# An explicit order of operations, bf16 loads and DMA transposes in an RWKV-7 scan with a feed-forward layer

## The chip, the cores and the metric

The kernel runs on one core of a Trainium2 chip. The metric is the device time of one execution in microseconds (us). "TensorE" below is the matmul engine (PE in the profile, PEld for its weight loads), VectorE is DVE, ScalarE is ACT, GpSimd is POOL, and SyncE is SP, which here only issues transfers. PSUM is where TensorE's results arrive; an "evacuation" is the copy of a result from there to SBUF, where the operands lie.

## The reference, cut to what matters

The first half is a recurrence over 768 steps with a 40x40 state for each of 4 x 8 heads. The second half sends the 3072 resulting rows through two matrices with a softplus between them.

```python
for t in range(S):                                   # S = 768, B = 4, H = 8, D = 40
    y[:, :, t] = np.einsum('bhd,bhde->bhe', rt, state)
    Sa = np.einsum('bhde,bhe->bhd', state, at)
    state = state * wt[:, :, None, :] - np.einsum('bhd,bhe->bhde', Sa, bt)
    state = state + np.einsum('bhd,bhe->bhde', vt, kt)
...
x = y.transpose(0, 2, 1, 3).reshape(B * S, H * D)    # 3072 x 320
h = x @ w_in                                         # 320 x 2048
g = np.maximum(h, 0.0) + np.log1p(np.exp(-np.abs(h)))
return g @ w_out                                     # 2048 x 320
```

## The kernel before

The sequence is cut into 12 chunks of 64 steps. Two chunks make a window. Per window a 32x32 triangular system per (head, parity) is inverted with elementwise operations (`invert`). Per chunk the operands are scaled, transposed, multiplied into Gram matrices and chained through the state (`second`); most of these are 64x64 matmuls (in the profile of this kernel 32 of them, at 207 us, take 0.37 us to the next group's start). Then come the feed-forward products with full 128x128 weights (`mlp`).

The program does not write instructions in a fixed order. It builds a graph of some 1,800 operations, and a greedy scheduler picks their order, engine and PSUM bank from modelled durations. One part of that model matters for this study, and I did not see that when I predicted: it has TensorE's instructions fetched in blocks of 256 (the profile below shows 63 instruction packets of 16 KB for 16032 TensorE instructions), and the scheduler charges for a block that arrives too late. The operations named in `SLOW` (feed-forward products, which are long for their instruction count: 0.11 us a matmul, start to start, at 204 us, where the 64x64 ones above take 0.012) are put where the model waits for a block.

```python
DVE_FW = (0, 1)                    # windows whose inverse runs on DVE, the others on GpSimd
BY_DMA = {"k": 99, "v": 99, "r": 99, ...}    # from which chunk on a transpose is made by DMA: never
...
BLOCK, AHEAD, FETCH, BEFORE = 256, 82, 2300.0, 70
SLOW = ("h", "o", "csb")

class Fetch:                       # the model of TensorE's instruction fetch
    def run(self, start, cost, n, keep=False):
        ...
        while left:
            edge = (at // BLOCK + 1) * BLOCK
            ask = edge - AHEAD
            ...
            if at == edge:
                w = max(0.0, asked + FETCH - t)      # the stall at the edge of a block
                stall += w
                t += w
...
# in schedule(): a stall is a penalty, and a long operation is wanted while a block is on its way
if e == "pe":
    pen += fetch.run(s + pen, c, 2 * COUNT[o.name])
    if o.name in SLOW:
        want = FILL if fetch.wants(s) else -SAVE
...
key = want - o.due - PEN * pen - 3.0 * cost * (len(o.engines) > 1)
```

A transpose is 8 matmuls of 128x128. The values v and r arrive as f32 over SyncE or ScalarE, and GpSimd casts them:

```python
def f(e):                          # transpose
    for bp in X2:
        for yy in range(H_ // 2):
            i = T.transpose(pb(t)[:, bp, off + 128 * yy:off + 128 * yy + 128],
                            src[:, bp, 128 * yy:128 * yy + 128], ident[:, :])
...
for n, dst, dn in (("v", v_, vn), ("r", r_, rn)):            # in second(c)
    src = RAW[n](c)[0]
    op(pool(640 * 0.85), landed(RAW[n], c), [dn],
       lambda e, dst=dst, src=src: P.tensor_copy(hd(dst), bh(src, D_)), name="cast")
turned(c, ("k", k_, [kn], kT_, kTn), ("v", v_, [vn], vT_, vTn))
turned(c, ("r", r_, [rn], rT_, rTn))
```

## Time and profile before

| | before |
|---|---|
| median of 3 runs | 351.06 us (348.99 to 351.34) |
| span of the profiled run | 345.8 us |
| first feed-forward matmul | 77.3 us |
| TensorE instructions (8016 matmuls, each with a weight load) | 16032 |

The prediction below shows the busy table, the table of stretches and the start. Four more lines of the page turned out to matter. They are the granted TensorE clock in 40 slices of the span (tenths of full speed), the DMA's busy share in the same slices, the queue of kind "instruction" (packets, MB, share of the 16 DMA engines), and the shares of the chain of work that ended last:

```profile
PEclk9967865569999978999899999999999999999999
DMA  8999984687667565676546465430411400100101
q8 instruction: 63, 1.03, 1.2%
PE 47%; ACT 11%; POOL 9%; DMA 9%; SPq 9%; DVE 7%; issue 5%; ACTq 2%; DVEq 0%; POOLq 0%
```

The clock is at 9 nearly everywhere from the tenth slice on. The third line is easily passed over, with 63 packets and 1.2% of the DMA. But 16032 TensorE instructions / 256 = 62.6, so I read these packets as TensorE's program arriving in blocks of 256 instructions (b_quart, further down, has 19488 / 256 = 76.1, and 76 packets). "issue" in the last line is time for which the profile names nothing to wait for. It is 5% of the chain here.

### The profile page before, as it was taken

Reading aid. Unit: us, or ns where it says so; the run is one execution under the profiler, and the core shown is the slowest. Engines: PE = TensorE matmul, PEld = TensorE weight load, DVE = VectorE, ACT = ScalarE, POOL = GpSimd, SP = SyncE. Lnnn points to the kernel's source line nnn. Section 1 sums busy time; section 2 is a strip of 40 time slices with the busy share of each in tenths; the row PEclk is TensorE's granted clock in tenths of the full one; section 3 lists DMA queues with packets and bytes.
Section 4 is the critical chain, followed back from the end, with each engine's and each line's share of the span. In section 5 each row is a group of like instructions: output and inputs, shape, how many; then the busy total and the mean of one; then the engine's idle time right before and its main releaser. Section 6 shows DMA issues by size and latency. Waiting matters only on the chain.

```text
span 345.8 us, 17638 instructions
## 1 busy us (share of the span) xinstructions
PE 280.4 (81%) x8016; PEld 212.7 (61%) x8016; DVE 232.7 (67%) x419; ACT 210.3 (61%) x296; POOL 169.2 (49%) x309
## 2 busy tenths in 40 slices
PE   0337247688789969999799999998989899999873
PEld 0226126576567747777577776786766678777642
DVE  7729978889997746657756697585885656664201
ACT  1246704226797825877568888667687368667661
POOL 8106000001000627898888788898888888000000
PEclk9967865569999978999899999999999999999999
DMA  8999984687667565676546465430411400100101
GB/s 134 171 174 142 182 159 79 107 145 113 122 120 156 103 112 94 123 126 108 102 79 104 83 104 96 78 69 14 89 34 21 91 14 13 33 6 21 39 22 38
DMA packets 145787, 31.30 MB, mean 90 GB/s; under 512 B 140272, under 2 KB 145392, under 8 KB 145712
## 3 DMA queue, kind: packets, MB, share of 16 engines
q1 hardware_dynamic: 129504, 25.09, 42.9%
q10 hardware_dynamic: 13728, 2.46, 5.1%
q0 software_dynamic: 2480, 2.62, 4.7%
q8 instruction: 63, 1.03, 1.2%
q14 instruction: 12, 0.10, 0.1%
HBM read 28.84 MB, written 3.93 MB: 95 GB/s over the span
## 4 chain that ended last, share of the span: by engine, by line
PE 47%; ACT 11%; POOL 9%; DMA 9%; SPq 9%; DVE 7%; issue 5%; ACTq 2%; DVEq 0%; POOLq 0%
PE ps L1205 12%; PE ps L1224 12%; SPq L664 8%; PE ps L730 7%; POOL mt L971 4%; DMA wout<-in_moe_w_out_dram 3%; POOL mtmp L967 3%; ACT gT L1214 3%; ACT et L1211 3%; PE ps L773 2%; DMA a_f<-in_a_dram 2%; PE ps L1073 2%; ACTq L664 2%; DMA r_f<-in_r_dram 2%; PE ps L1174 2%
## 5 line engine op out<-in xcount | busy, mean ns | idle before, releaser
L1205 PE MATMUL ps<-xT,win 128*128 128x256 bf16 x576 | 79.9, 275 | 3.5 <-ACT et L1211 1.8
L1211 ACT ACTIVATE et<-ps 128x512 f32<-128x512 f32 x96 | 57.2, 596 | 36.3 <-PE ps L1205 35.8
L967 POOL TENSOR_TENSOR mtmp<-mt 128x30 f32<-128x30 f32 (+14 forms) x120 | 60.5, 504 | 33.0 <-DVE mt L960 24.3
L971 POOL TENSOR_TENSOR mt<-mt,mtmp 128x30 f32<-128x30 f32 (+14 forms) x120 | 66.8, 557 | 8.7
L1224 PE MATMUL ps<-wout,gT 128*128 128x320 bf16 x384 | 65.2, 302 | 5.9 <-ACT gT L1214 2.9
L1205 PEld LDWEIGHTS ps<-xT,win 128*128 128x128 bf16 x576 | 50.6, 98 | 15.9 <-ACT et L1211 6.0
L1214 ACT ACTIVATE gT<-et,hln 128x1024 bf16<-128x1024 f32 x48 | 55.2, 1151 | 1.4
L1224 PEld LDWEIGHTS ps<-wout,gT 128*128 128x128 bf16 x384 | 34.2, 98 | 20.1 <-ACT gT L1214 4.6
L1035 POOL CAST r_b<-r_f 128x640 bf16<-128x640 f32 x12 | 9.5, 789 | 44.2 <-DMA r_f<-in_r_dram 39.6
L1035 POOL CAST v_b<-v_f 128x640 bf16<-128x640 f32 x12 | 9.2, 765 | 37.0 <-DMA v_f<-in_v_dram 24.8
L1229 DVE TENSOR_TENSOR osb<-ps,csb 128x320 f32<-128x320 f32 x24 | 11.6, 484 | 20.3 <-PE ps L1224 20.1
L785 DVE TENSOR_TENSOR qt<-ps,sut 128x1024 bf16<-128x1024 f32 x12 | 14.6, 1221 | 5.6 <-PE ps L773 5.6
L814 PE MATMUL ps<-lw,nexc 64*64 64x320 bf16 x96 | 7.2, 361 | 13.8 <-ACT lw L845 13.6
L814 PE MATMUL ps<-lw,ninc 64*64 64x320 bf16 x96 | 9.8, 328 | 8.5 <-ACT ginv L862 6.2
L785 DVE TENSOR_TENSOR tak<-ps,sut 128x1024 bf16<-128x1024 f32 x12 | 14.6, 1219 | 2.8 <-PE ps L773 2.6
L785 DVE TENSOR_TENSOR pt<-ps,sut 128x1024 bf16<-128x1024 f32 x12 | 14.6, 1216 | 2.6 <-PE ps L773 2.6
L1180 DVE TENSOR_TENSOR yo<-ps,gexc 128x640 bf16<-128x640 f32 x12 | 9.9, 821 | 8.3 <-PE ps L1174 8.2
L845 ACT ACTIVATE lw<-w_f 128x1280 bf16<-128x1280 f32 x6 | 7.7, 1282 | 12.3 <-DMA w_f<-in_w_dram 12.3
L868 DVE TENSOR_TENSOR kh<-k_f,ginv 128x640 bf16<-128x640 f32 x12 | 10.9, 910 | 4.8 <-DMA k_f<-in_k_dram 4.8
L985 ACT ACTIVATE dex<-dc,blk 128x1024 bf16<-128x1024 bf16 x6 | 6.9, 1146 | 11.6 <-DVE dc L979 11.6
L866 DVE SCALAR_TENSOR_TENSOR nh<-b_f,ginv 128x640 bf16<-128x640 f32 x12 | 9.9, 825 | 5.3 <-ACT ginv L862 5.3
L862 ACT ACTIVATE ginv<-ps 128x640 f32<-128x640 f32 x12 | 8.4, 704 | 8.0 <-issue 6.8
(152 smaller groups left out, 587.9 us busy)
## 6 DMA issues: line engine op xcount, KB each, us to landing
out_dram<-osb SPq DMA_DIRECT2D x48, 80.0 KB, 2.3
b_f<-in_b_dram SPq DMA_DIRECT2D x44, 80.0 KB, 3.6
v_f<-in_v_dram SPq DMA_DIRECT2D x44, 80.0 KB, 3.3
a_f<-in_a_dram SPq DMA_DIRECT2D x44, 80.0 KB, 3.4
k_f<-in_k_dram SPq DMA_DIRECT2D x44, 80.0 KB, 3.6
r_f<-in_r_dram SPq DMA_DIRECT2D x42, 80.0 KB, 3.1
w_f<-in_w_dram SPq DMA_DIRECT2D x20, 160.0 KB, 4.2
wout<-in_moe_w_out_dram POOLq DMA_DIRECT2D x4, 320.0 KB, 10.0
```

The source lines that it names most:

```text
L664: lambda e, bp=bp, x=x, q=q: queue(e).dma_start(heads(t[q:q + 64, bp, :], D_), SRC[n][2 * bp + x][:, c * L:(c + 1) * L, :].rearrange("h p ...
L730: i = T.transpose(pb(t)[:, bp, off + 128 * yy:off + 128 * yy + 128], src[:, bp, 128 * yy:128 * yy + 128], ident[:, :])
L785: lambda e: V.tensor_tensor(parity(dst), bh(pf(t), L), bc4(mask[:, :], L), ALU.mult), name="mask")
L814: i = T.matmul(pf(t)[s:s + 64, bp, 0:DM], mats[z][q:q + 64, :], heads(lwt[q:q + 64, bp, :], 2 * D_)[:, :, z * D_:z * D_ + D_], start=(z == ...
L967: lambda e, j=j, nt=nt, tv=tv: E_.tensor_tensor(tv, m[:, 0:j, j:j + 1].to_broadcast([128, j, nt]), m[:, j:j + 1, j + 1:32].to_broadcast([1 ...
L971: lambda e, j=j, tv=tv: E_.tensor_tensor(m[:, 0:j, j + 1:32], m[:, 0:j, j + 1:32], tv, ALU.add),
L1035: lambda e, dst=dst, src=src: P.tensor_copy(hd(dst), bh(src, D_)), name="cast")
L1205: i = T.matmul(one(t)[:, 256 * (q % 2):256 * (q % 2) + 256], win[:, z, q * 128:(q + 1) * 128], xT_[:, z, :], start=(z == 0), stop=(z == 2))
L1211: lambda e, q2=q2, t=t, ett=ett: A.activation(ett[:, q2 % 2, :], one(t), AF.Exp), name="exp")
L1214: lambda e, q2=q2, ett=ett: A.activation(gts[q2 // 2][0][:, :, :].rearrange("p q m -> p (q m)"), ett[:, :, :].rearrange("p q m -> p (q m)" ...
L1224: i = T.matmul(one(t)[:, 0:DM], gts[z][0][:, q % 4, bp * 128:(bp + 1) * 128], wout[:, q, :], start=(q == 0), stop=(q == NQ - 1))
L1229: lambda e, t=t, ot=ot: V.tensor_tensor(ot[:], one(t)[:, 0:DM], csb[:], ALU.add), name="oe")
```

## The change

The intent is to take work off TensorE (transposes by DMA, cheaper transposes, fewer switches between 64x64 and 128x128 mode), to take the casts off GpSimd by letting its DMA cast, to share the inverses between GpSimd and DVE, and to replace the greedy scheduler by an explicit order found by a local search. The scheduler goes, and its model of instruction fetch goes with it; whether the search had such a model, the file does not say.

```diff
-DVE_FW = (0, 1)
+DVE_FW = (0, 1, 3, 5)
-FIRST = [...]; BY_ACT = (...); TUNED = {...}      # (cut)
-BY_DMA = {"k": 99, "v": 99, "r": 99, "u": 99, "a": 99, "n": 99}
+BY_DMA = {"k": 4, "v": 4, "r": 4, "u": 99, "a": 99, "n": 99}
+ORDER = (2, 110, 3, 70, 32, 33, ...)              # 1792 numbers (cut)
+ENGINE = "..."; BANK = "..."                      # (cut)
+QUARTERS = "101011111111111010111100111111111101111011111100"
...
-class Fetch: ...
-def schedule(ops): ...
+def arrange(ops):
+    for o, q in zip((o for o in ops if o.alt), QUARTERS):
+        o.mode = o.alt[0] if q == "1" else o.mode
+    for at, n in enumerate(ORDER):
+        o = ops[n]
+        o.eng = names[ENGINE[n]]
+        ...                                        # PSUM banks from BANK (cut)
+    return [ops[n] for n in ORDER]
...
-        r_b = Ring("r_b", 1, [128, 2, 512], BF)
+        r_b = Ring("r_b", 2, [128, 2, 512], BF)
...
+        def load_cast(n, c):                       # v and r, by GpSimd, f32 -> bf16
+            ...
+                    op({"pool": 700.0}, [], [nm + "%d%d" % (bp, x)],
+                       lambda e, bp=bp, x=x, q=q: P.dma_start(
+                           heads(t[q:q + 64, bp, :], L)[:, :, 0:D_],
+                           SRC[n][2 * bp + x][:, c * L:(c + 1) * L, :].rearrange("h p d -> p h d")),
+                       dma=(nm + "%d%d" % (bp, x), 512))
...
         def transpose(src, srcs, t, off):
+                        for q in (0, 64) if mode == QUAD else ():
+                            for o in (0, 64):
+                                i = T.transpose(pb(t)[o:o + 64, q // 64, n:n + 64],
+                                                src[q:q + 64, bp, 128 * yy + o:128 * yy + o + 64], eye(q))
```

A "quarter" transpose is thus 32 matmuls of 64x64 where a "whole" one is 8 of 128x128. Of the 48 transposes left on TensorE, 38 are by quarters. The two counts that follow from this are 8736 matmuls instead of 8016, and 171 mode switches instead of 243.

> **What bounds the kernel now.** I read the page's busy table first, then the table of stretches, then the timeline of the start and of a stretch in the middle.
>
> The busy table: TensorE (PE) is the busiest engine, and no other is near it.
>
> ```profile
> PE 280.4 (81%) x8016; PEld 212.7 (61%) x8016; DVE 232.7 (67%) x419; ACT 210.3 (61%) x296; POOL 169.2 (49%) x309
> ```
>
> The table of stretches (start:end, length, busy time of each engine, granted clock, DMA share, GB/s) shows that this average hides two regimes. I cut the span where the first matmul of the feed-forward part (L1205) starts, at 77.3 us, and where the tail begins.
>
> ```profile
> 0.00:40.00 40.00, 15.20 (x304) 10.57 (x304) 28.37 (x93) 17.55 (x23) 14.54 (x39) 0.87 1.12 158
> 40.00:77.00 37.00, 23.31 (x766) 18.70 (x768) 31.25 (x64) 10.22 (x13) 2.17 (x3) 0.58 0.77 127
> 77.00:320.00 243.00, 224.44 (x6782) 171.82 (x6767) 169.74 (x258) 170.49 (x245) 152.50 (x267) 0.98 0.45 80
> 320.00:346.00 26.00, 17.47 (x191) 11.60 (x188) 3.35 (x6) 12.03 (x16) 0.00 (x0) 0.97 0.15 33
> ```
>
> In the first 77 us PE is busy 38.5 us and idle as long; VectorE (DVE) is busy 59.6 of 77 and the DMA is saturated until 40. From 77 to 320 us PE is busy 224 of 243 us: here the time is PE's own work plus 18.6 us of gaps. The tail of 26 us is the last chunk's exp, ln and output product in turn.
>
> The timeline of PE and of DVE at the start tells what the first part waits for.
>
> ```profile
> 36.17 1.96 DVE L960 STREAM_TRANSPOSE mt<-mc 128x1024 f32<-128x1024 f32 x1
> 43.82 4.21 PE L705 MATMUL ps<-wout,ones 128*128 128x320 bf16 x16 [5.62 <-DMA wout<-in_moe_w_out_dram]
> 50.14 1.04 DVE L979 STREAM_TRANSPOSE dc<-mb 128x512 f32<-128x512 f32 x1
> 52.41 0.64 PE L926 MATMUL ps<-ident,dex 64*64 64x64 bf16 x32 [4.39 <-ACT dex L985]
> 77.34 0.83 PE L1205 MATMUL ps<-xT,win 128*128 128x256 bf16 x6
> ```
>
> The inverse of the first window, which every later step needs, starts only at 36.2 us (the transpose of mc on DVE) and ends at 51; PE meanwhile stands in front of the column sums of w_out, whose load was issued only at 29.5 us. Three things made it late. ScalarE, whose queue also issues loads, sat 6.8 us in front of "ginv" behind five loads. Chunk 2 was prepared before the inverse. And the loads of chunks 2 and 3 stood among those of 0 and 1 (b1, v0, a0, a1, w2, k0 on the sync queue), with the DMA full.
>
> [...] Start to start, from the timeline at 204 us:
>
> ```profile
> 204.55 0.83 PE L1205 MATMUL ps<-xT,win 128*128 128x256 bf16 x6
> 205.21 1.25 PE L1224 MATMUL ps<-wout,gT 128*128 128x320 bf16 x8
> 206.30 0.82 PE L1205 MATMUL ps<-xT,win 128*128 128x256 bf16 x6
> 207.05 0.44 PE L1082 MATMUL ps<-v_b,tak 64*64 64x40 bf16 x32
> ```
>
> The same six matmuls take 0.66 us when the next group is 128*128 and 0.75 us when it is 64*64: a switch costs about 0.09 us. [...] No transposing DMA runs in the kernel before, so its time is not in the trace. [...] one 64x64 copy on DVE takes 1.22 us while GpSimd runs the fmask select (5.2 us into the run) and 0.17 us at 8.4 us.
>
> **The change part by part.** Counts are from the comparison of the two instruction orders.
>
> *Transposes out of PE.* k, v and r of chunks 4 to 11: 24 transposes of 8 matmuls go to DMA. One takes 0.45 us start to start at full clock (201.27 to 201.72 in the timeline), so 24 x 0.45 = 10.8 us leave PE, all after the first L1205. Their evacuations leave too (DVE 0.69, ACT 1.02 us each).
>
> *Transposes by quarters.* Of the 48 left, 38 become 32 matmuls of 64x64. The quarters of L926 take 0.28 us start to start (96.29 to 96.57), so each saves 0.16 to 0.17; 25 of them lie after the first L1205: 4.0 us.
>
> *Mode switches.* On PE 243 become 171, after the first L1205 220 become 164: 56 x 0.09 to 0.1 = 5.3 us.
>
> Together 20.1 us of PE work leave the PE-bound stretch.
>
> *The start.* The new order loads k0, a1, w0, a0, b0, b1 first, has ScalarE issue fewer loads before ginv, works chunks 0 and 1 through first, and puts the inverse of window 0 before chunk 2. Seven sets of four loads (these six and v0) stand before the last scaled operand. A load is 512 packets; queue 1 spent 42.9% of 16 x 345.8 us on 129504 packets, or 18.3 ns each, so 0.59 us of all 16 engines: 28 x 0.59 = 17 us. Scaling, transposes, their evacuations (4 x 0.69) and mc then put the transpose of mc at about 24 us instead of 36. The inverse took 15.0 us (36.2 to 51.2) and is as long: about 39.5 instead of 52 us. From there before takes 25 us to the first L1205, with DVE busy 17.5 of 20 us. In the new order DVE has 17.8 us of work between those points, counted by the durations of before (5 masks of 1.22, 2 more under omask, 2 additions into dex of 1.21, and so on), and some 3 us of waits: first L1205 at about 60 us, 17 us earlier. Seven PE operations fewer precede it (45 against 52), which is 2.5 us of work to be done later. w_out is issued after nh1 (near 13 us) and took 14 us from issue to last landing before, so I expect it before 39.
>
> *v and r as bf16 by GpSimd.* 24 casts (18.7 us of GpSimd) go; 96 DMAs come. The four w_out DMAs of 512 packets were issued at 0.75 us each: 96 x 0.75 = 72 us of GpSimd. The waits of GpSimd on r_f and v_f (39.6 and 24.8 us) go with the casts. HBM still reads f32, so no bytes are saved there.
>
> *Inverses of windows 3 and 5 from GpSimd to DVE.* GpSimd took 127 + 11 us for four windows, so 69 us go; GpSimd's busy time falls to about 169 - 69 - 19 + 72 = 153 us. DVE gets 2 x 60 operations. By the window-0 durations (0.19 us at 28 elements, 0.27 at 112: 0.16 us + 1.0 ns per element) a window of 9,920 elements costs 60 x 0.163 + 9.8 = 19.6 us, two 39 us. Against it stand 24 evacuations of transposes and 20 chain evacuations that leave DVE or move to ACT (16.5 + 9.7 us), so DVE rises from 233 to about 251 us.
>
> *Sum.* Span 345.8 - 17 + 2.5 - 20.1 = 311 us. DVE then has about 202 us of work between 60 and 289 us, 88%, where it had 70%; PE will wait for it now and then. I add 6 us, my choice: span 317. The measured median lies 5.2 us over the profiled span now, so 322 us.
>
> **The rivals.**
> 1. *DVE becomes the bound.* For it: 88% with two chains of 60 dependent operations each; between 77 and 100 us, where DVE was at 21.5 of 23, PE was at 18.6 of 23. Against: GpSimd and DVE inverses alternate in the new order (window 4's mt comes as window 3 ends)[...], and the order was searched with DVE in view. If PE falls to 85% in two stretches of 45 us, add 6 more: 330 to 335.
> 2. *DMA transposes or GpSimd loads arrive late.* [...] SyncE issues them in order with loads and outputs, and already waited 62 us for osb, so one late transpose holds loads behind it. GpSimd's loads stand in order with its inverse and wait for the two v_b buffers; a cast of 160-byte pieces may cost more than 18.3 ns. If it shows it is as gaps in front of grams from chunk 4 on: 330 to 345.
> 3. *The early part stays DMA-bound.* 6.4 MB came in the first 40 us at 158 GB/s. If w_out lands late, it still holds PE and the start gains 5 us, not 17: 334.
> 4. *The search also closes gaps.* 18.6 us between 77 and 320 and the tail are there to gain: 305 to 312.
>
> **Range and chances.** The PE part (20 us) is nearly sure as work; whether it reaches the end depends on rivals 1 and 2. The start (about 15 us) is likelier than not. Without one of the two the time is 334 to 340, still more than 2% (7 us) faster; both must fail, or a new wait must eat them, for "same". So 322 us, range 304 to 339; faster 0.92, same 0.05, slower 0.03.
>
> **What would show it.** PE busy near 250 us; first L1205-kind matmul near 60 us; first transpose of mc near 24; switches cheaper in sum; no feed-forward gap on a transposing DMA longer than 1 us; DVE near 250 busy. It would be wrong if the first feed-forward matmul came after 70 us, if PE were under 88% between it and the tail, or if gaps named the DMA into kT, vT, rT or v_b.

## The result, and the profile after

The prediction was wrong, in direction too. Ratios here and below are the mean time of one kernel's fast runs over that of the other's in the same rounds, so not quite the ratio of the medians quoted.

| | before | after |
|---|---|---|
| median in the same rounds | 351.20 us | 366.03 us (361.54 to 369.86, 4 runs, 2 in the slow state) |
| ratio, 95% interval | | 1.0332 (1.0233 to 1.043): slower |
| span of the profiled run | 345.8 us | 366.7 us (slow state) |

Since that profile fell in the slow state, I ran the changed kernel again ("a_again"): 360.84 us (359.59 to 362.53), ratio 1.0365, with a profiled run in the fast state of span 359.6 us. Its profile is read from here on as that of "after". (In its rounds only three of before's seven runs are in the fast state, so its interval is wide: 1.0228 to 1.0501.) The page:

```profile
PE 273.4 (76%) x8736; PEld 202.7 (56%) x8736; DVE 252.5 (70%) x502; ACT 211.7 (59%) x312; POOL 148.2 (41%) x259
PEclk9985558555995889999878679999999999999999
DMA  9989995482799165839998988699873829423012
q0 software_dynamic: 53168, 6.56, 29.7%
q8 instruction: 68, 1.11, 1.3%
PE 50%; DVE 20%; ACT 13%; issue 10%; DMA 5%; SPq 1%; POOL 1%; DVEq 0%; POOLq 0%; ACTq 0%
```

DVE and GpSimd are busy for as long as predicted (251 and 153 us). TensorE's busy time fell by 7 us only, although the work that was to leave did leave. The clock row is 5 in seven of the first 13 slices, and dips to 6 and 7 again between the 21st and the 24th, where before was at 9. "issue" is 10% of the chain instead of 5%, and instruction packets are 68 instead of 63 (17472 instructions / 256 = 68.25).

The table of stretches of after, with the columns that the prediction explains, cut where the first feed-forward matmul starts:

```profile
0.00:40.00 40.00, 9.83 (x200) 5.96 (x200) 25.70 (x86) 12.62 (x16) 20.56 (x50) 0.79 1.21 150
40.00:78.00 38.00, 21.05 (x1007) 16.94 (x1007) 27.94 (x52) 13.64 (x19) 8.11 (x13) 0.59 0.82 97
78.00:320.00 242.00, 208.45 (x7005) 155.02 (x7001) 186.43 (x343) 162.66 (x247) 119.56 (x197) 0.91 0.79 93
320.00:360.00 40.00, 34.06 (x540) 24.80 (x537) 12.46 (x22) 22.79 (x31) 0.00 (x0) 1.00 0.19 39
```

Between 78 and 320 us TensorE is busy 208 of 242 us, where it was busy 224 of 243 before. The DMA share there is 0.79 instead of 0.45, and the clock 0.91 instead of 0.98.

**A budget.** I cut the span at the first feed-forward matmul. From there to TensorE's end I counted three things. "Half clock" is the time lost to it, an estimate: a weight load takes 95 to 115 ns at full clock and some 150 at half (means in before: 98 to 108 ns by group at 200 to 208 us, where the granted clock was 1.00, and 141 to 154 at 60 to 68 us, where it was 0.50), so half of the distance to the next load is counted as lost (0.6 us of distance at most) for each load of 118 ns or more. (The granted clock of the same stretch, 0.98 and 0.92 on average, gives nearly the same: 5.1 and 22.2 us.) "Gaps" are all the time in which neither TensorE nor its weight loads are busy. "Work" is what remains. "issue" pauses, here and below, are TensorE's waits of over 0.15 us to which the profile gives that name (the lines "<- issue" of `prof LABEL --waits --engine PE`, summed). The last column puts the prediction's sum in the same form: its 6 us of allowance for waits on DVE are gaps.

| us | before | after | difference | predicted difference |
|---|---|---|---|---|
| first feed-forward matmul | 77.3 | 78.0 | +0.7 | -17 |
| work at full clock | 237.1 | 221.7 | -15.4 | -17.6 |
| lost at half clock | 4.7 | 21.3 | +16.6 | 0 |
| gaps (of these "issue") | 23.2 (4.1) | 35.0 (13.5) | +11.8 (+9.4) | +6 |
| TensorE's end to the end | 3.5 | 3.5 | 0 | 0 |
| span | 345.8 | 359.6 | +13.8 | -28.6 |

The work left TensorE as predicted. Three other rows ate it: the start did not come forward, TensorE ran longer at half clock, and gaps grew. Most of that growth is "issue".

**The start of after**, first DVE. Columns: start, duration, engine, line, operation, tiles, count, and in brackets the idle time before it and what ended it.

```profile
27.98 1.90 DVE L876 STREAM_TRANSPOSE mt<-mc 128x1024 f32<-128x1024 f32 x1
40.77 0.83 DVE L780 TENSOR_TENSOR ah<-a_f,gexc 128x640 bf16<-128x640 f32 x1 [7.54 <-DMA a_f<-in_a_dram]
53.60 0.88 DVE L903 TENSOR_SCALAR dex<-dc,blk 128x1024 bf16<-128x1024 bf16 x2
```

The inverse starts at 28.0 us (before 36.2; I predicted 24). But the order puts chunk 2's scaling of a into the middle of the inverse. DVE works in order and stands 7.5 us for that load, the last of whose four parts was issued at 27.3 us and landed at 40.7. So the inverse is through at 53.6 us and not at 39.5. Then TensorE, from the same view:

```profile
44.38 0.34 PE L689 MATMUL ps<-nT,aT 40*64 40x64 bf16 x6
48.55 0.58 PE L689 MATMUL ps<-nT,aT 40*64 40x64 bf16 x26 [3.82 <-issue]
59.68 0.35 PE L859 MATMUL ps<-gT 64*64 64x64 bf16 x21 [1.53 <-issue]
63.68 0.46 PE L963 MATMUL ps<-dex,tlo 64*64 64x32 bf16 x21 [1.54 <-issue]
72.62 0.51 PE L1046 MATMUL ps<-kh,v_b 64*64 64x40 bf16 x22 [2.67 <-issue]
78.00 1.46 PE L1120 MATMUL ps<-xT,win 128*128 128x256 bf16 x6
```

The first two lines are the clue. One operation of 32 matmuls, all of them released by the same semaphore, stops after 6 and goes on 3.8 us later. No data can explain that. The same happens four times before the first feed-forward matmul, 9.6 us in all, and that group of six then takes 1.46 us where it took 0.83 in before: the clock is at half (granted 0.50 from 70 to 80 us in a_again; 1.00 from 77 to 79 us in before).

**Where these pauses are.** I numbered TensorE's instructions in order, with its own semaphore and drain instructions (85 in the trace). In both profiles of the changed kernel the longer "issue" pauses stand in front of the same numbers: 706, 1217, 1473, 1986, 2497, 2753, 3778, 4034, 4289 and so on. Each is 193 or 194 more than a multiple of 256. The same holds for all seven "issue" pauses of before, and for 348 of the 350 in the 20 profiles of this study. So the pauses stand at the edges of blocks of 256 instructions, and the packets have one size (1.11 MB in 68 packets is 16.3 KB each). The cost is not small: the "issue" pauses sum to 23.4 us over the whole of a_again, against 4.1 in before.

### The profile page after: what moved, and what is told of

The parts are those of the page before. It is cut to its first block, busy times and chain, and to the rows that moved or that the text cites. A ratio compares the mean times of both kernels' runs of the same rounds, so it can differ in the third digit from the quotient of the medians.

```text
span 366.7 us, 19068 instructions
## 1 busy us (share of the span) xinstructions
PE 276.4 (75%) x8736; PEld 205.0 (56%) x8736; DVE 252.5 (69%) x502; ACT 212.1 (58%) x312; POOL 148.6 (41%) x259
## 3 DMA queue, kind: packets, MB, share of 16 engines
q8 instruction: 68, 1.11, 1.3%
## 4 chain that ended last, share of the span: by engine, by line
PE 51%; DVE 16%; ACT 14%; issue 10%; DMA 6%; SPq 1%; DVEq 0%; ACTq 0%
PE ps L1120 14%; PE ps L1139 11%; ACT gT L1129 5%; PE ps L689 4%; ACT et L1126 4%; DMA a_f<-in_a_dram 4%; PE ps L637 3%; PE ps L730 3%; PE ps L1046 2%; PE ps L986 2%; PE ps L1087 2%; DMA vT<-v_b 2%; SPq L556 1%; DVE ninc L481 1%; DVE pt L701 1%
## 5 line engine op out<-in xcount | busy, mean ns | idle before, releaser
L1120 PE MATMUL ps<-xT,win 128*128 128x256 bf16 x576 | 85.7, 289 | 3.3 <-ACT et L1126 2.4
L1120 PEld LDWEIGHTS ps<-xT,win 128*128 128x128 bf16 x576 | 53.7, 102 | 18.9 <-ACT et L1126 7.4
L579 POOL DMA_DIRECT2D v_b<-in_v_dram x48 | 33.6, 718 | 55.6 <-PE ps L1046 20.9
L579 POOL DMA_DIRECT2D r_b<-in_r_dram x48 | 33.9, 724 | 51.8 <-PE ps L637 40.7
L883 POOL TENSOR_TENSOR mtmp<-mt 128x30 f32<-128x30 f32 (+14 forms) x60 | 31.9, 532 | 26.1 <-DVE mt L876 11.1
L887 POOL TENSOR_TENSOR mt<-mt,mtmp 128x30 f32<-128x30 f32 (+14 forms) x60 | 32.6, 544 | 4.0
L1146 DVE TENSOR_TENSOR osb<-ps,csb 128x320 f32<-128x320 f32 x24 | 11.7, 486 | 21.3 <-PE ps L1139 19.6
L730 PE MATMUL ps<-lw,nexc 64*64 64x320 bf16 x96 | 6.9, 360 | 23.4 <-DVE nexc L485 16.0
L887 DVE TENSOR_TENSOR mt<-mt,mtmp 128x30 f32<-128x30 f32 (+14 forms) x60 | 19.8, 330 | 1.6
L883 DVE TENSOR_TENSOR mtmp<-mt 128x30 f32<-128x30 f32 (+14 forms) x60 | 19.7, 329 | 1.6
L780 DVE TENSOR_TENSOR ah<-a_f,gexc 128x640 bf16<-128x640 f32 x12 | 10.9, 905 | 9.2 <-DMA a_f<-in_a_dram 7.3
L797 ACT ACTIVATE mc<-ps,blk 128x512 f32<-128x512 f32 x12 | 8.1, 688 | 13.4 <-PE ps L689 13.4
L701 DVE TENSOR_TENSOR tak<-ps,sut 128x1024 bf16<-128x1024 f32 x12 | 14.6, 1217 | 1.4 <-PE ps L689 1.0
```

The costliest lines, as they stand in the source:

```text
L579: lambda e, bp=bp, x=x, q=q: P.dma_start(heads(t[q:q + 64, bp, :], L)[:, :, 0:D_], SRC[n][2 * bp + x][:, c * L:(c + 1) * L, :].rearrange(" ...
L701: lambda e: V.tensor_tensor(parity(dst), bh(pf(t), L), bc4(mask[:, :], L), ALU.mult), name="mask")
L730: i = T.matmul(pf(t)[s:s + 64, bp, 0:DM], mats[z][q:q + 64, :], heads(lwt[q:q + 64, bp, :], 2 * D_)[:, :, z * D_:z * D_ + D_], start=(z == ...
L883: lambda e, j=j, nt=nt, tv=tv: E_.tensor_tensor(tv, m[:, 0:j, j:j + 1].to_broadcast([128, j, nt]), m[:, j:j + 1, j + 1:32].to_broadcast([1 ...
L887: lambda e, j=j, tv=tv: E_.tensor_tensor(m[:, 0:j, j + 1:32], m[:, 0:j, j + 1:32], tv, ALU.add),
L1120: i = T.matmul(one(t)[:, 256 * (q % 2):256 * (q % 2) + 256], win[:, z, q * 128:(q + 1) * 128], xT_[:, z, :], start=(z == 0), stop=(z == 2))
```

## The experiments

Theories at this point, which the texts on record weigh under these or shorter names:

- **Crowded DMA:** the instruction packets are DMA traffic like the data (q8 takes 1.3% of the 16 engines in a_again). The DMA share rose to 0.79, so blocks come late. Then a lighter DMA brings them back in time, and traffic added to the kernel before makes such pauses.
- **Hungry program:** quarter transposes turn 8 matmuls into 32, and an order with long runs of 64x64 matmuls uses up 256 instructions faster than a block can be fetched. Then the pauses stay with a light DMA, and go with the quarters or with the order.
- **Start:** the start was lost to the order of DVE's work alone, and a better order there gains some 12 us.
- **One bad part:** one of the parts costs in itself, whatever the order (casting loads, DMA transposes, the inverses on DVE).

### Is it the DMA?

**a_light**: the changed kernel; from chunk 2 on, each casting load brings one head of eight (wrong on purpose from there).

```diff
-    heads(t[q:q + 64, bp, :], L)[:, :, 0:D_],
-    SRC[n][2 * bp + x][:, c * L:(c + 1) * L, :].rearrange("h p d -> p h d")),
+    heads(t[q:q + 64, bp, :], L)[:, 0:1 if c >= 2 else 8, 0:D_],
+    SRC[n][2 * bp + x][0:1 if c >= 2 else 8, c * L:(c + 1) * L, :].rearrange("h p d -> p h d")),
```

> The kernel after, but from chunk 2 on each casting load of v and r brings one head of eight (64 packets in place of 512); same instructions, order and semaphores; wrong result on purpose. It takes 80 x 448 packets x 32 ns / 16 = 72 us of all-engine DMA away, most of it from 20 to 250 us. Theory A (the full DMA delays TensorE's instruction fetches, and the gaps cool its clock): gaps of TensorE put down to 'issue' fall from 28 us to under 15, the clock of 60 to 220 us comes back above 0.9, and the time is 345 to 355 us. Rival B (the order itself costs: in-order stalls on DVE and TensorE): time stays within 1.5% of the kernel after, 357 to 366 us, the gaps stay.

**a_trlight**: the changed kernel; each DMA transpose moves one 128x128 block of eight (wrong on purpose).

```diff
-    out=dst[:, :, :].rearrange("p b (y m) -> p (b y) m", m=128),
-    in_=src[:, :, :].rearrange("p b m -> p (b m)"))
+    out=dst[:, :, :].rearrange("p b (y m) -> p (b y) m", m=128)[:, 0:1, :],
+    in_=src[:, 0, 0:128])
```

> The kernel after, but each transposing DMA turns one 128x128 block of eight; wrong result on purpose. It takes 24 x 7/8 x 2.3 = 48 us of all-engine DMA away, from about 100 us on. Theory A: the clock from 180 to 220 us (0.57 to 0.74) comes back above 0.9, issue gaps after 150 us go, time 350 to 358 us; nothing changes before 77 us. Rival B: 360 to 366 us.

**a_bothlight**: both edits (wrong on purpose).

> Both lightenings at once; wrong result on purpose. The DMA share falls from about 81% to under 50%. Theory A: issue gaps under 10 us in all, clock near 0.97 after 80 us, the time 330 to 343 us, that is faster than before, since the 20 us of TensorE work that the change took away then show. Rival B: 357 to 366 us. Rival C (DVE is the bound after 60 us): 350 to 360 us with the gaps of TensorE named DVE in place of issue.

**b_traffic**: the kernel before, with four extra loads of 512 packets into an unused buffer behind each of the 48 outputs, issued by SyncE.

```diff
             ins = o.fn(o.eng)
             ...
+            if extra: extra()     # after an output: four S.dma_start(scratch, v ...), each with its own semaphore
```

> The kernel before with 192 added loads of 512 packets into a tile that nobody reads, four behind each output on the sync queue, so from about 105 us on; 192 x 512 x 16.3 ns / 16 = 100 us more of all-engine DMA, right result. Theory A: issue gaps of TensorE grow from 4 us to over 10, its clock falls in places, the time is 355 to 370 us. Rival B: the DMA was at 45% there and has room; the time stays within 1% of 351 us (or the sync queue's own order delays a load, and then gaps name a DMA into a tile and not issue).

The three kernels that are wrong on purpose passed the comparison with the reference all the same, so it does not see these values here; only their times are used. All other kernels of this study are right by construction and passed. Measured (before in these rounds 349.85 us):

| kernel | median us | ratio to before (95%) | "issue" pauses us |
|---|---|---|---|
| a_light | 355.20 | 1.0200 (1.0132 to 1.0269) | 18.5 |
| a_trlight | 360.46 | 1.0364 (1.0263 to 1.0465) | 18.3 |
| a_bothlight | 355.14 | 1.0158 (1.0057 to 1.0259) | 19.5 (slow profile) |
| b_traffic | 405.39 | 1.1589 (1.1473 to 1.1704) | 2.8 |

The comparison to make is with a_again (1.0365, other rounds, so the step between them is good to about one per cent). The pauses stay in place with the data traffic taken away: the DMA share between 78 and 320 us is 0.79 in after, 0.55 in a_light and 0.36 in a_bothlight (0.45 in before), and the sums are 23.4, 18.5 and 19.5 us (4.1). In the timeline of TensorE of a_light, the first and the last of those shown above are there again:

```profile
47.45 0.58 PE L689 MATMUL ps<-nT,aT 40*64 40x64 bf16 x26 [3.70 <-issue]
70.90 0.51 PE L1046 MATMUL ps<-kh,v_b 64*64 64x40 bf16 x22 [2.38 <-issue]
```

And b_traffic, whose DMA carried 192 loads more (share 0.65 in the same stretch), had 2.8 us of "issue" pauses, fewer than before itself. It was slowed by something else: outputs and loads queued behind the dummy loads (SyncE's queue and the DMA are 33% of its chain).

The packed traces also hold each instruction packet, which no view lists singly. The median packet took 0.98 us in before, 0.97 in a_again, 0.97 in a_light, 0.98 in b_traffic and 1.04 in b_burst (below), where the DMA is idle but for them. So crowded DMA does not make these pauses, and that theory fell. What the lighter casting loads gained, about 1.5% or 5 us, is small, and the intervals of the two ratios overlap; lightening the transposes alone gained nothing that the interval can tell. (Of the forecasts, only rival B's for a_trlight was met. a_light fell between the two ranges, a_bothlight had the time of rival C but not its gaps, and b_traffic was slower than both.)

### Is it the quarters, or the start?

**a_again**: the changed kernel as it is.

> The kernel after, unchanged: control of the next three on the same chip and a profile of the fast state. Ratio to before 1.02 to 1.04; gaps of TensorE put down to 'issue' 20 to 28 us, each at the same places of TensorE's instruction stream (every one on a boundary of 256 instructions) as in the three lightened kernels.

**a_whole**: the changed kernel with every transpose on TensorE whole: 15648 instructions instead of 17472, and 195 mode switches instead of 171.

```diff
-QUARTERS = "101011111111111010111100111111111101111011111100"
+QUARTERS = "000000000000000000000000000000000000000000000000"
```

> The kernel after with all 38 transposes by quarters made whole again (8 matmuls of 128x128 in place of 32 of 64x64); order, engines and transfers as after. TensorE has 1824 instructions fewer (15648 in place of 17472, 61 fetches in place of 68), but 38 x 0.16 = 6 us more matmul work and 24 more mode switches (195 for 171), 2.2 us. Theory F (instructions reach TensorE in blocks of 256, one every 3.3 us or more, and stretches of 64x64 matmuls use a block in 1.2 to 2 us, so TensorE starves at block boundaries): issue gaps fall from some 20 to under 12 us, the clock of 40 to 220 us recovers, the time is 3 to 12 us below after. Rival Q (the quarters save what the prediction counted and the order's other waits cost): the time is 5 to 8 us above after.

**a_start**: the changed kernel; in `ORDER` the two scalings, transposes and the Gram product of chunk 2 stand behind the inverse of window 0, and the column sums of w_out come before chunk 2's first transposes.

> The kernel after with its start reordered: the two scalings of chunk 2, their transposes and gram come behind the inverse of window 0 (on VectorE and TensorE), and the column sums of w_out before TensorE's first transposes of chunk 2. It removes VectorE's stall of 7 us in the inverse, on the load of a of chunk 2. Theory S (the stall in the in-order queue is what the start lost): the expanded inverse (dex) comes at 46 in place of 53 us, the first feed-forward matmul (L1120) at 70 to 72 in place of 77, the time is 5 to 7 us below after. Rival F2 (TensorE's start is instruction-starved): the first feed-forward matmul moves by under 3 us, since the four gaps of 1 to 4 us between 44 and 72 stay, and the time by under 3 us.

**a_startwhole**: both.

> Both edits. If they add up under theories F and S: 8 to 18 us below after, 343 to 354 us, which is near before. If F is right and S wrong: as a_whole within 3 us.

**a_start2**: all transposes whole, and the same parts of chunk 2 spread along the first chunk's chain instead of put in one place.

> As a_startwhole (whole transposes; chunk 2 behind the inverse of window 0), but the parts of chunk 2 are spread along the first chain (scalings behind its first masks, transposes behind its second products, gram behind U), and the column sums of w_out stand behind the first transposes of k and v. In a_start the inverse did come 11.6 us earlier (41.5 in place of 53 us), but TensorE then stood 7 us in front of chunk 2's evacuations. Theory S (the start's loss is order alone): first feed-forward matmul at 66 to 70 us, time 345 to 350. Rival (TensorE's half clock and its fetch gaps hold the chain): first feed-forward matmul at 72 to 75, time 352 to 356.

**a_hwstart**: a_start2, with v and r loaded as f32 over SyncE and cast by GpSimd as in before.

> As a_start2, but v and r come as float32 over SyncE's queue and GpSimd casts them, as before: 49152 packets of 16 to 18 ns in place of 32 ns, which takes 40 us of all-engine DMA and 72 us of DMA issuing on GpSimd away and puts 24 casts of 0.8 us back. Right result. If the light loads told the truth (7 us for the whole of v and r), 3 to 6 us below a_start2: 341 to 350 us. If not: within 2 us of a_start2, or above it where SyncE's queue blocks.

| kernel | median us | ratio to before (95%) | first feed-forward matmul | "issue" pauses us |
|---|---|---|---|---|
| a_again | 360.84 | 1.0365 (1.0228 to 1.0501) | 78.0 | 23.4 |
| a_whole | 355.95 | 1.0231 (1.0124 to 1.0339) | 74.6 | 9.9 |
| a_start | 367.23 | 1.0461 (1.0223 to 1.07) | 79.6 (slow profile) | 22.5 (slow profile) |
| a_startwhole | 362.14 | 1.0378 (1.0243 to 1.0514) | 79.7 | 9.5 |
| a_start2 | 363.79 | 1.0396 (1.032 to 1.0472) | 77.9 | 17.8 |
| a_hwstart | 383.06 | 1.0900 (1.0792 to 1.1007) | 78.4 (slow profile) | 13.6 (slow profile) |

a_whole is the cleaner result. It gives 6.7 us of work back to TensorE (228.4 us at full clock from the first feed-forward matmul on, against 221.7) and still is 4.9 us faster (same rounds, all eight runs fast, no overlap). Two rows of the budget pay for that: the half-clock loss falls from 21.3 to 12.5 us, and the first feed-forward matmul comes 3.4 us earlier. The "issue" pauses more than halve, in that stretch from 13.5 to 6.7 us, but its gaps sum to 35.0 us as before: other waits took their place. In its page TensorE is busier than in after, at fewer instructions:

```profile
PE 275.5 (78%) x7824; PEld 206.7 (58%) x7824; DVE 252.8 (71%) x502; ACT 211.5 (60%) x312; POOL 148.6 (42%) x259
```

The start experiments missed. In a_start the inverse is through at 41.5 us, 12 us earlier than in after and close to the 39.5 that I had predicted, and yet the first feed-forward matmul comes no earlier (nor in a_startwhole, whose profile is fast). TensorE's timeline shows what stood there instead:

```profile
51.99 0.38 PE L845 MATMUL ps<-ident,dex 64*64 64x64 bf16 x13 [2.73 <-issue]
65.03 0.64 PE L640 MATMUL ps<-ident,ah 64*64 64x64 bf16 x32 [3.36 <-ACT gT L449]
```

Chunk 2's transposes now stand in the in-order queue of TensorE ahead of chunk 0's last steps and wait there for evacuations, and pauses of 2.7, 1.8 and 2.7 us remain. So the late inverse alone does not explain the late start: removed in this way, it is replaced by the next wait. a_hwstart was much slower. What TensorE waits for beyond a_start2 is GpSimd's cast into v_b (11.9 us at a time) and, early on, 12.1 us instead of 6.3 for "lw" on ScalarE; I moved the casts by a simple rule only, so it tells little about the loads. I did not pursue it, and whether hardware-issued loads would suit the new order is open.

### What does a block of instructions cost?

**b_burst**: the kernel before, with a tail on TensorE alone, after all other engines are done: 32 whole transposes, 32 by quarters, 32 whole, then 16 times (12 feed-forward matmuls and one quarter transpose). The data is in place, and nothing evacuates, so only TensorE's own speed and its instructions are left. (One look, 435.6 us; its total is not compared.)

```diff
+        def tail():
+            whole(32)
+            quarter(32)
+            whole(32)
+            return mixed(16)
+        emit(nc, st, order, tail)
```

> The kernel before, and behind its last output TensorE alone runs 32 whole transposes (8 matmuls of 128x128 each), 32 transposes by quarters (32 matmuls of 64x64 each, 2048 instructions with the weight loads), 32 whole ones again, and 16 times (12 feed-forward matmuls, then one transpose by quarters). No other engine and almost no transfer runs beside it; the result is right. Theory F: the quarters start at 0.28 us each and then stall at every block of 256 instructions: 8 blocks of 3.3 us or more, so 26 to 30 us for the stretch of 32, 0.8 to 0.9 us per transpose, more than a whole one (0.45 to 0.56 us); whole ones have no stall, and in the mixed stretch the quarters cost 0.28 us again. Rival (the gaps come from the crowded DMA or from other engines): the stretch of quarters takes 32 x 0.28 = 9 us.

```profile
346.11 14.47 PE L1285 MATMUL ps<-ident,kh 128*128 128x128 bf16 x256 [0.59 <-DVE osb L1234]
360.51 1.08 PE L1296 MATMUL ps<-ident,kh 64*64 64x64 bf16 x109
361.93 1.24 PE L1296 MATMUL ps<-ident,kh 64*64 64x64 bf16 x128 [0.34 <-issue]
365.67 1.93 PE L1296 MATMUL ps<-ident,kh 64*64 64x64 bf16 x128 [2.51 <-issue]
369.69 1.92 PE L1296 MATMUL ps<-ident,kh 64*64 64x64 bf16 x128 [2.09 <-issue]
...
388.42 0.48 PE L1296 MATMUL ps<-ident,kh 64*64 64x64 bf16 x19 [2.10 <-issue]
406.22 0.45 PE L1296 MATMUL ps<-ident,kh 64*64 64x64 bf16 x32
```

This is the mechanism laid bare. The 32 whole transposes run without a pause: 14.47 / 32 = 0.45 us each, as the prediction had it, or 7.2 us for 256 instructions. The first 109 quarter matmuls run at full speed. Then TensorE executes exactly 128 matmuls, which are 256 instructions, and waits, again and again. Seven blocks take 388.42 - 361.93 = 26.5 us, or 3.8 us per block (3.5 to 4.0), and a quarter transpose (a quarter of a block) costs **0.95 us** in such a run instead of 0.31 from its busy time (1.24 / 4). It is not the cheaper form then but twice as dear as a whole one. The last line is a quarter transpose alone between feed-forward matmuls: 0.38 us from its start to the next group's, switch included, which is cheaper than whole.

What a block waits for can be read from the instruction packets of these seven. From TensorE's start on one block to the start of the packet for the next pass 1.1 to 1.7 us, the packet takes 0.9 to 1.4, and TensorE starts 1.4 to 1.5 us after the packet's end. The last piece is the mark of a fetch: over before, a_again, a_light, a_bothlight, b_traffic, b_burst, b_quart and c_order3, all 167 "issue" pauses at an edge of a block end 1.1 to 1.8 us after an instruction packet landed.

There is a second effect in these lines. After the first long pause a block takes 1.92 us where it took 1.24: the clock is at half (granted 1.00 from 361 to 365 us, 0.50 from 365.2 to 392), and stays there with pauses of only 1.5 to 2.5 us every 3.5 to 4 us. One pause of 0.34 us did not do that.

**b_quart**: the kernel before in exactly its order, written out as a list, with all 72 transposes by quarters and nothing else.

```diff
+QUARTERS = '1' * 72
```

> The kernel before in exactly its own order, banks and engines, but all 72 transposes by quarters: 3456 TensorE instructions more, 76 fetched blocks in place of 63; TensorE's work falls by 72 x 0.16 = 11.5 us and it has fewer mode switches; right result. As the prediction counted: 12 to 18 us faster than before, 333 to 340 us. Theory F: the issue gaps grow from 4 us to 25 or more and the clock falls with them, so the time is 355 to 370 us.

It took 387.20 us, ratio 1.1060 (1.0961 to 1.1158). The page:

```profile
PE 287.2 (75%) x9744; PEld 209.4 (54%) x9744; DVE 233.5 (61%) x419; ACT 212.7 (55%) x296; POOL 169.3 (44%) x309
q8 instruction: 76, 1.25, 1.3%
```

By the prediction's arithmetic 72 quarters at a gain of 0.16 us save 11.5 us of TensorE. Instead the kernel is 35.9 us slower than before in the same rounds (351.33), with 45.8 us of "issue" pauses instead of 4.1. (Theory F, the hungry program, had forecast 355 to 370 us: the direction was right, the size too small.) DVE, ScalarE and GpSimd did the same work in the same time, and the DMA carried the same data. With that the hungry program is shown: more 64x64 instructions in a fixed order are enough to make the pauses.

### Does one of the other parts cost in itself?

Each was put alone into before's own order, written out. (Before's scheduler itself got stuck when one part was changed; no run on record shows that.)

**b_inv**: inverses of windows 3 and 5 on DVE.

```diff
-DVE_FW = (0, 1)
+DVE_FW = (0, 1, 3, 5)
```

> The kernel before in its own order, but the 120 steps of the inverses of windows 3 and 5 (and their last two operations) run on VectorE in place of GpSimd, at the same places of the order. GpSimd loses 69 us, VectorE gains 40 (233 to 272 busy, since its evacuations are not moved to ScalarE as in after). The prediction's rival 1: VectorE nears its bound, and TensorE waits for it in the stretches of the two inverses, +6 us or more, 357 to 365. Other theory: the inverse is off the critical path on either engine: within 1% of 351.

**b_tr**: k, v and r transposed by DMA from chunk 4, each issued as soon as its data is there. Destinations keep one buffer each.

```diff
-BY_DMA = {"k": 99, "v": 99, "r": 99, "u": 99, "a": 99, "n": 99}
+BY_DMA = {"k": 4, "v": 4, "r": 4, "u": 99, "a": 99, "n": 99}
```

> The kernel before in its own order, but k, v and r of chunks 4 to 11 are transposed by DMA: 24 transposes of 0.45 us and their evacuations leave, 24 transposing DMAs of 2.3 us of all engines (4.7 us from issue to landing) come, each issued as early as its inputs and its single destination buffer allow. As the prediction counted: 10.8 us of TensorE, 340 to 344 us. Rival D: the destinations have one buffer, so vT and rT can be asked for only when the chunk before has read them, and TensorE waits 1 to 4 us in each of 8 chunks for v and r (gaps named DMA into vT or rT): 355 to 370 us.

**b_cast**: v and r by casting loads of GpSimd, two buffers for r_b, no casts; `load_cast` as in the diff of the change.

> The kernel before in its own order, but v and r come as casting loads by GpSimd: 24 casts (19 us) leave GpSimd, 96 issues of 0.75 us come, 49152 packets of 32 ns in place of 16. As the prediction counted: no loss, within 1% of 351 us or a little faster. Theory D (the crowded DMA and GpSimd's in-order queue, where a load waits for its buffer before the inverse may go on): 355 to 370 us, with GpSimd's inverses later and gaps named GpSimd, DMA or issue on TensorE.

| kernel | median us | ratio to before (95%) | from first feed-forward matmul to TensorE's end: work, half clock, gaps (us) |
|---|---|---|---|
| before | 350.67 | | 237.1, 4.7, 23.2 |
| b_inv | 360.36 | 1.0340 (1.0258 to 1.0421) | 238.9, 7.3, 28.0 |
| b_tr | 371.90 | 1.0524 (1.0389 to 1.0658) | 225.1, 22.1, 46.6 (slow profile) |
| b_cast | 371.45 | 1.0639 (1.0571 to 1.0707) | 234.9, 10.9, 42.0 |

None has more "issue" pauses at the edges of blocks than before (2.3, 4.0 and 3.6 us), so none of these parts is the source of those. b_tr does take 12 us of work off TensorE, and gives them back: 17.6 us of TensorE's pauses wait for rT to land from a DMA transpose, and the half clock follows. In b_cast GpSimd becomes the chain, as four inverses and 96 issues stand in one queue:

```profile
POOL 44%; PE 26%; DVE 11%; issue 6%; ACT 5%; DMA 5%; ACTq 1%; POOLq 1%; DVEq 0%
```

In the changed kernel GpSimd has two inverses less, and no TensorE gap among those listed names a DMA. These three results therefore say what a part costs in an order made for something else, and no more. (Of the forecasts, rival 1 came out in b_inv, and D, about, in b_tr and b_cast.) They leave one question: do the parts work together, in an order that knows about the blocks?

### The same parts in another order

**c_order1, c_order2, c_order3**: exactly the operations, engines and transfers of the changed kernel, with new `ORDER` and `QUARTERS` tables (`BANK` and `ENGINE` keep their contents). I found them by a local search on a model fitted to the traces above. It assumes that a block of 256 TensorE instructions takes 3.6 to 4 us to fetch (3.5 to 4.0 per block in b_burst), one at a time; that TensorE's clock falls after idling (from 1.00 to 0.50 in b_burst, in the pause of 2.5 us) and recovers after work (from 0.50 at 60 to 66 us to 1.00 at 77 to 79 in before); and that other operations and transfers take what they took in these traces. For c_order3 the search went on from c_order1, with durations up to 8% and transfers up to 2 us worse at random. (That model is not a measurement, and nothing is concluded from its times.) Quarters: 21, 19 and 20 of 48; mode switches 205, 215 and 197.

```diff
-ORDER = (2, 110, 3, 70, ...)
+ORDER = (...)                        # the same 1792 operations
-QUARTERS = "101011111111111010111100111111111101111011111100"
+QUARTERS = "011011101111000001010001110101000101110000000000"     # that of c_order3
```

> The same operations, engines and transfers as the kernel after (DMA transposes, casting loads, inverses of windows 3 and 5 on VectorE), 21 of 48 transposes by quarters, in another order. My model of the traces puts after at 363, its own best order at 320. Theory O (the parts are good, the order starved TensorE): issue gaps under 8 us, 320 to 340 us, faster than before. Rival (the parts cost whatever the order, as each did alone in before's order): 350 us or more.

> As c_order1, from another start of the search and with 19 transposes by quarters; the model says 326. Theory O: 325 to 345 us; rival: 350 us or more. Two orders show whether one result is luck.

> The same operations, engines and transfers as after and c_order1, 20 of 48 transposes by quarters, in an order searched on from c_order1 under the harder model, which puts c_order1 at 362 and this at 332 (both too high or low by the same bias, so -8%). Theory O (order is what is left): 325 to 340 us. Rival (c_order1's remaining gaps are not what the model thinks): within 1% of c_order1, 343 to 350 us.

| kernel | median us (runs) | before in the same rounds | ratio to before (95%) |
|---|---|---|---|
| c_order1 | 346.17 (20) | 348.71 | 0.9901 (0.9866 to 0.9935) |
| c_order2 | 351.10 (17) | 348.71 | 1.0066 (1.0024 to 1.0108) |
| c_order3 | 343.27 (4) | 350.36 | 0.9832 (0.9753 to 0.9911) |

c_order3, the best of three, is 1.7% below before in four fast runs: clear of 1, but unclear against the 2% that verdicts here ask for. It can't be told from c_order1 (1.0% below). All three missed the 320 to 345 us that theory O had forecast; c_order3 fell in its rival's range. Against the changed kernel (1.0365 of before, in other rounds) c_order3 is about 5% faster, with the same operations, engines and transfers: only the order and the form of 24 of the 48 transposes (18 fewer by quarters) differ. Page, stretches and first feed-forward matmul of c_order3:

```profile
PE 272.3 (80%) x8304; PEld 203.1 (60%) x8304; DVE 251.1 (74%) x502; ACT 214.1 (63%) x312; POOL 152.3 (45%) x259
PEclk9999999956999899989996999999999999999999
```

```profile
40.00:64.00 24.00, 16.26 (x742) 13.40 (x733) 20.04 (x31) 10.63 (x15) 4.65 (x7) 1.00 0.65 95
64.00:320.00 256.00, 226.20 (x7060) 170.19 (x7049) 194.15 (x360) 176.67 (x264) 126.88 (x202) 0.95 0.80 94
```

```profile
64.05 0.83 PE L1123 MATMUL ps<-xT,win 128*128 128x256 bf16 x6
```

The first feed-forward matmul comes at 64.1 us, 13.3 earlier than in before, at full clock. So most of the early start that I predicted exists. The inverse is through at 41.1 us (DVE has no wait of over 0.15 us between 25 and 45 us), and the first feed-forward matmul follows 23.0 us later, about as in after (24.4): this order gains the earlier inverse without the new waits of a_start. The rest of the budget, in the form used above, is 229.8 us of work, 11.3 at half clock and 31.8 of gaps (16.6 of them "issue"), against 237.1, 4.7 and 23.2 of before: 7.3 us of work saved, 6.6 + 8.6 lost, 7.9 us net loss. The gain over before is the start. What the parts save on TensorE, even this order gives back as pauses and half clock. The DMA share in the main stretch is 0.80 (0.79 in after), so these transfers leave room for a faster kernel.

One thing here speaks against too simple a story. Over the whole run the "issue" pauses of c_order3 sum to 21.0 us, hardly less than the 23.4 of after, and those of c_order1, which is no faster, to 10.4 (slow profile). A pause costs its length only where nothing else would have held TensorE anyway: in a_whole "issue" fell from 13.5 to 6.7 us in that stretch, and the gaps still summed to 35.0. What c_order3 has less of than after, in the main stretch, is half clock (11.3 us against 21.3) and other gaps (15.2 against 21.5); what it has more of is work (229.8 against 221.7), since fewer transposes are by quarters.

## Why the prediction was wrong, point by point

The profiled span was 42.4 us above the predicted one (359.6 against 317.2). By the budget 17.7 of these are the start, 16.6 the half clock, 5.8 gaps beyond the 6 allowed, and 2.2 work. So two steps of its sum failed: the start's -17, and the missing term for a TensorE that is starved of instructions and runs at half clock. Two of its own three signs of being wrong came true: the first feed-forward matmul after 70 us, and PE at 86% (208 of 242 us) where 88 was the bound.

- **What left TensorE.** Right. I predicted a net -17.6 us after the first feed-forward matmul; at full clock it was -15.4. The counts and 0.45 us per whole transpose held.
- **"so each saves 0.16 to 0.17" (transposes by quarters).** This is the step in which the fetch was overlooked, though not the largest loss. The 0.28 us were taken from an L926 group that was not starved. In b_burst a quarter transpose takes 0.38 us between feed-forward matmuls, and 0.95 us in a run of its own kind. In the changed kernel they bring 1824 more TensorE instructions (912 matmuls), and undoing them alone gained 4.9 us. I read neither the instruction queue's line of the page nor the class in the code whose only purpose was this wait, and the change took that class out.
- **The sum "345.8 - 17 + 2.5 - 20.1".** It has no term for time that TensorE spends neither working nor waiting for data. That missing term measured +9.4 us of "issue" pauses in the main stretch. It also has no term for the clock, although I had quoted the 0.58 of before's start. That one measured +16.6 us, an estimate from weight loads. Together they are more than the 15.4 us that the work saved.
- **"first L1205 at about 60 us, 17 us earlier".** Wrong: 78.0. "About 39.5 instead of 52" failed first (53.6), because DVE stood 7.5 us for chunk 2's load in the middle of the inverse; I had summed DVE's work in that stretch but not checked when that load is issued. a_start repaired that step (41.5) and nothing was gained, since other waits took its place. Of the 18 us, 14.1 lie before the end of the inverse and 3.9 after it (24.4 us to the first feed-forward matmul where the sum had 20.5). c_order3, at 64.1, shows that most of the 17 us was within reach of these parts, though not of that order.
- **"I add 6 us" for waits on DVE.** Not needed for DVE: after the first feed-forward matmul, TensorE's waits of over 0.15 us that name DVE went from 8.8 to 9.1 us. Gaps in all rose by 11.8 us there, 9.4 of them "issue". (The sum for DVE's busy time is also off: 233 + 39 - 16.5 - 9.7 is 246 and not 251; measured 252.5.)
- **The sizes of the transfers (rival 2's figures).** The casting loads were mis-sized. Comparing q0 of a_again and a_light, 29.7% and 11.6% of 16 engines' spans, 35,840 packets fewer saved 1,053 us, or 29 ns each, where I had reckoned with 18.3 and only feared more. For the transposes the kernel before gave no time to go by: in b_tr q1 took 53.9% of its 16 x 376.2 us, in before 42.9% of 16 x 345.8, so 24 transposes cost 870 us, 2.3 us of all 16 engines each. Casting loads and transposes together made the DMA share 0.79, and a_bothlight (1.0158 against 1.0365, with intervals that overlap) puts what that cost in time at some 2%.
- **Rivals.** Rival 1 (DVE the bound) was not it, and rival 2's sign hardly showed: no wait of TensorE in a_again names a DMA, and in the slow profile a single one of 1.2 us does (vT). Rival 3 guessed an early part bound by loads; it was one late load of chunk 2, in front of the inverse, and not w_out. (By rival 1's own 6 us the time is 328, not 330 to 335.) None of the four was the fetch of instructions.
- **"both must fail, or a new wait must eat them".** The form of the argument was sound, the weight was not. The start failed mostly through the order on DVE, and the work saved was eaten by new waits and the clock; 0.03 for "slower" was far too little. (Without the 20 us of work its own figure is 342, outside its range.)

**What stays open.** How the loss splits between the order, the quarters and the clock can't be told exactly, since the clock fell in a pause (to 0.50 in the one of 2.51 us in b_burst) and the pauses were shorter at that clock (1.55 to 2.10 us, blocks of 1.92 us instead of 1.24); a_whole gives the quarters 4.9 us in after's order, and c_order3 gives order and quarters together some 5%. The half-clock rows come from one execution each, and a lower clock need not cost time: of the 15 fast runs of c_order1, six had a mean granted clock of 0.88 to 0.89 and took 343.9 us on average, nine had 0.95 to 0.985 and took 345.1. Of the 3.5 to 4 us per block only some 1 us is the packet; what fills the time before and after it is not shown. Whether each of the other parts pays in an order made for it was not tried.

## What to carry to other kernels

Count the instructions of the busiest engine as well as its time: replacing few long matmuls by many short ones paid here only while the surrounding work used up 256 instructions more slowly than a block arrived (3.8 us in b_burst; whole transposes took 7.2 us for 256 instructions and ran without a pause, quarter ones 1.24 and paused), so put long 128x128 products between runs of 64x64 ones. Before removing a part of a scheduler, ask what each term of its cost model was paying for. When pauses carry no named cause and cut one operation in two, number the instructions in front of them before suspecting the data.
